# A state-space scan and its feed-forward on one core: the factors of the first pair, the scan and the decay matmuls put elsewhere

## The chip, the core and the metric

The kernel runs on one NeuronCore of a Trainium2 chip. A core has a matrix engine (TensorE, PE in the profile), a vector engine (VectorE, DVE), an activation engine (ScalarE, ACT), a general engine (GpSimd, POOL) and a queue engine (SyncE, SP). Each has its own instruction stream and they meet only at semaphores. Data lies in SBUF (128 partitions); matmul results go to PSUM, in eight banks. Loads and stores are DMAs that SP, ACT or POOL issue.

The metric is the device time of the whole kernel in microseconds (us): the median of eight runs.

## The reference

Two layers follow each other. The first is a chunked state-space recurrence over 4 batches of 8 heads, 768 steps, head size D = 32, state size N = 16. With `cum` the running sum of `log a` inside a chunk:

```python
L = np.exp(cum[:, :, :, None] - cum[:, :, None, :]) * causal
M = np.einsum('bhin,bhjn->bhij', Cc, Bc) * L
y = einsum('bhij,bhjd->bhid', M, xc) + einsum('bhin,bhnd->bhid', Cc, state) * np.exp(cum)[..., None]
state = decay_full * state + sum_j Bc[j] x[j] * decay_from_j[j]
```

Its output, 3072 tokens of 256 channels, goes through a gated feed-forward with 1536 hidden channels:

```python
gate = np.maximum(x @ w_gate, 0.0)
val = x @ w_val
return (gate * val) @ w_out
```

## The kernel before, in words

**Decays as factors.** The kernel does not form `L`. It takes running products of `a` (`cp0` for batch 0, `cp` for all batches), multiplies C by the product at its own step and B by its inverse, so that C times B carries the ratio. `factors()` (L213) turns `cp0`, one row per head and chunk of 128 steps, into a PSUM tile `fac` with steps on partitions, by matmuls against parts of the identity. L772 copies it to SBUF as `wfac[:, 1]` (the factors of C); reciprocals give `wfac[:, 0]` (the factors of B), pair 0 in L778, pairs 1 and 2 in L784. These serve batch 0.

For batches 1 to 3 `scan()` (L236) runs the products of all batches over half a sequence (384 steps) on VectorE. `middle()` (L242) takes the reciprocal of the product at half time, into `pick`. `decay()` (L249) turns it over: eight matmul records for the first pair of batch 1 (`dec3`, L257) and six for the rest (L262), in one PSUM bank; a float32 matmul is two records. `decay_factors()` (L269) copies the result to SBUF on ScalarE (`fac3`, `scaleBC`).

**Pairs and blocks.** Work on the recurrence goes by pairs of 128-step chunks, 256 tokens, three pairs to a batch, twelve in all. A pair's steps are: load B, C, x; scale B and C by the factors (`scale_wide`, L303; L322 is its product); transpose both on TensorE (`transp`); evacuate them as BT and CT (`tevac`, L369; CT is L385 on ScalarE or L388 on VectorE); multiply (`G_wide`, L411: 16 small matmuls into four PSUM banks); mask on VectorE (`gmask`, L433) with ScalarE copies (`gcopy`, L437); sum states (`adds`, `carry`, `pass_on`); multiply with state and x (`inter_wide` L498, `D_wide` L523); evacuate to `yT` (`yevac_wide`, L540). The feed-forward goes by blocks of 512 tokens, two pairs. `gvh` (L677) does one group of 128 hidden channels for half a block (four matmuls, L686; relu on ScalarE, L689; product on VectorE in `finish`, L692), `gv` (L663) one group for a whole block (L668, L671, L674, L675), `fout` (L699) the output matmuls (L713). `keep_warm` (L186) issues matmuls into a spare bank that nobody reads.

**PSUM banks.** The pool tag "shared" has five banks, used in turn. `gvh` takes one, `G_wide` four, `gv` two. A bank is free again when the last reader of its contents is done: for `gvh(..., True)` that is the `finish` that is called later in the program.

**Order.** The order of each engine is the order of the program: `in_order` (L15) ties every instruction to the one before it on its engine. The beginning of the program is therefore a hand-written order: pair 0 as fast as its inputs allow, pair 1 behind it, and from L838 on `gvh` groups of block 0 in between. The weights come through Pool's DMA queue in pieces of 128 hidden channels times two; their first issue waits for a one-element memset of `wg` on VectorE (L773). Between these issues Pool also scales pair 1 (L786, L787). Input loads are issued on SP and on ACT, in the order in which they are written (L132 to L144).

The stretch from L825 on, where the decay matmuls stand:

```python
f0 = gvh(0, 0, 0, True)
G_wide(1)
decay()
adds(1)
gcopy(1, 0)
gmask(1, 2, V, True)
f0()
```

Of the kernel before, what the change touches and what calls it, by code (L numbers as in the profile page):

```python
# [8 lines left out]
FP32 = mybir.dt.float32  # L9
# [20 lines left out]
def kernel(  # L30
# [13 lines left out]
    nc = tc.nc  # L44

    NB, NH, S, D = x.shape
# [15 lines left out]
    mm = ctx.enter_context(tc.tile_pool(name="mm", bufs=1, space=bass.MemoryType.PSUM))  # L62
# [14 lines left out]
    st = {}  # L77

    def load_bc(p, j, *qs):
        s = st.setdefault(p, {})  # L80
        if "bcr" not in s:
            s["bcr"] = raw.tile([128, NH, 2, 2, N], FP32, tag="bcr", name="bcr")
            if p == 2:
                nc.vector.memset(s["bcr"][0:1, 0, 1, 0, 0:1], 0.0)
        b, s0 = p // PPB, p % PPB * 256
        n = NH // len(qs)
        for i, q in enumerate(qs):
            hs = slice(i * n, (i + 1) * n)
            q.dma_start(
                out=s["bcr"][:, hs, j].rearrange("p h r n -> p h (r n)"),  # L90
                in_=(B, C)[j][b, hs, s0:s0 + 256, :].rearrange(
                    "h (p r) n -> p h (r n)", r=2))

    def load_x(p, *qs):
        xr = raw.tile([128, NH, 2, D], FP32, tag="xr", name="xr")
        if p == 2:
            nc.vector.memset(xr[0:1, 0, 0, 0:1], 0.0)
        b, s0 = p // PPB, p % PPB * 256
        n = NH // len(qs)
        for i, q in enumerate(qs):  # L100
            hs = slice(i * n, (i + 1) * n)
            q.dma_start(out=xr[:, hs].rearrange("p h r d -> p h (r d)"),
                        in_=x[b, hs, s0:s0 + 256, :].rearrange(
                            "h (p r) d -> p h (r d)", r=2))
        st.setdefault(p, {})["xr"] = xr
# [23 lines left out]
    H = S // 2  # L129
    HC = NC // 2  # L130
# [5 lines left out]
    nc.vector.memset(first, 0.0)  # L136
    load_bc(0, 1, nc.sync, nc.scalar)
    load_bc(0, 0, nc.sync, nc.scalar)
    a_sb = glob.tile([2 * BH, H], FP32)
    nc.sync.dma_start(out=a_sb, in_=a.rearrange("b h (w s) -> (b h w) s", w=2))  # L140
    load_x(0, nc.sync, nc.scalar)
    load_bc(1, 1, nc.sync)
    load_bc(1, 0, nc.scalar)
    load_x(1, nc.sync)  # L144
    nc.scalar.activation(first[:, 1:2], first[:, 0:1], AF.Relu)
# [9 lines left out]
    for rows, base in ((slice(0, 128), 128), (slice(0, 64), 0)):  # L155
        nc.gpsimd.affine_select(
            out=wmask[rows], in_=wmask[rows], pattern=[[-1, 2], [1, 128]],
# [28 lines left out]
    def keep_warm(n, rhs=warm):  # L186
        w = bank("w", (128, 128))
        for _ in range(n):
            nc.tensor.matmul(out=w, lhsT=warm, rhs=rhs, start=True, stop=True)  # L189
# [5 lines left out]
    def weights(f0, f1, which=(0, 1)):  # L195
        fs = slice(f0 * 128, f1 * 128)
        for j in which:
            w, src = ((wg, moe_w_gate), (wv, moe_w_val))[j]
            nc.gpsimd.dma_start(  # L199
                out=w[:, :, fs], in_=src[:, fs].rearrange("(k p) f -> p k f", k=2))  # L200
# [10 lines left out]
    dec = glob.tile([128, NC], FP32)  # L211

    def factors():  # L213
        d = bank("fac", (128, 2, NH, PPB))
        for r in range(2):
            for i in range(2):
                nc.tensor.matmul(
                    out=d[64 * i:64 * i + 64, r].rearrange("p h k -> p (h k)"),
                    lhsT=cp0[:, r:128:2], rhs=idr[:, i:R:2], start=(r == 0), stop=True,
                    tile_position=(0, 64 * i), skip_group_check=True)  # L220
        return d
# [3 lines left out]
    def decays(step):  # L225
        if step == 0:
            nc.vector.tensor_scalar_mul(ends, onew, cp0[:, 127:128])
            return
        d = bank("dec", (128, NC))
        nc.tensor.matmul(out=d, lhsT=heads.rearrange("p q t n -> p (q t n)"), rhs=ends,  # L230
                         start=True, stop=True)
        nc.scalar.copy(out=dec, in_=d)
# [3 lines left out]
    def scan(s0, s1):  # L236
        nc.vector.tensor_tensor_scan(
            out=cp[:, s0:s1], data0=a_sb[:, s0:s1],
            data1=zero1.to_broadcast([2 * BH, s1 - s0]),
            initial=cp[:, s0 - 1:s0] if s0 else 1.0, op0=ALU.mult, op1=ALU.add)  # L240

    def middle():  # L242
        nc.vector.reciprocal(rmid, cp[:, H - 1:H])
        nc.vector.tensor_scalar_mul(pick[:, 0], pairs[:, 0], rmid)

    fac3 = glob.tile([128, 2, 2, NH], FP32)
    scaleBC = glob.tile([128, NB, NC, 2, 8], FP32)

    def decay():  # L249

        bank_ = mm.tile([128, HC * 2 * NB * 8 + 16], FP32, tag="tp", name="dec")
        n = HC * 2 * NB * 8
        d = bank_[:, 0:n].rearrange("p (k w b h) -> p k w b h", k=HC, w=2, b=NB)
        st["dec3"] = d3 = bank_[:, n:n + 16].rearrange("p (r h) -> p r h", r=2)
        for r in range(2):
            for i in range(2):
                nc.tensor.matmul(  # L257
                    out=d3[64 * i:64 * i + 64, r], lhsT=cp[:, i * 128 + r:i * 128 + 128:2],
                    rhs=pick[:, 0, NH:2 * NH], start=(r == 0), stop=True,
                    tile_position=(0, 64 * i), skip_group_check=True)  # L260
        for k in range(HC):
            nc.tensor.matmul(  # L262
                out=d[:, k].rearrange("p w b h -> p (w b h)"),
                lhsT=cp[:, k * 128:(k + 1) * 128],
                rhs=pick.rearrange("p w h -> p (w h)"),
                start=False, stop=True, skip_group_check=True)
        st["dec"] = d

    def decay_factors():  # L269
        d = st["dec"]  # L270
        nc.scalar.copy(out=fac3[:, 1], in_=st["dec3"])
        for w in range(2):
            cs = slice(w * HC, (w + 1) * HC)
            nc.scalar.copy(
                out=scaleBC[:, :, cs, 1, :].rearrange("p b k h -> p k b h"), in_=d[:, :, w])

    def inverse(b0, b1):
        for b in range(b0, b1):
# [24 lines left out]
    def scale_wide(p, j, eng):  # L303
        s = st[p]
        if p >= FIRST:
            s["bs"] = bs = tok[p % NTOK]
            src = s["bcr"].rearrange("s (t q) j r n -> s j r t q n", t=2)[:, j]
            for t in range(2):
                k = 2 * j * (1 + t)
                eng.tensor_tensor(  # L310
                    out=bs[:, k:k + 2].rearrange("s k (q t n) -> s k t q n", q=4, t=2)[:, :, t],
                    in0=src[:, :, t],
                    in1=fac3[:, j, :, 4 * t:4 * t + 4].to_broadcast([128, 2, 4, N]),
                    op=ALU.mult)
            return
        if "bs" not in s:
            s["bs"] = bs = att.tile([128, 4, 128], BF16, tag="bs", name="bs")
            s["tin"] = [[bs[:, 2 * j + r] for r in range(2)] for j in range(2)]
        src = s["bcr"].rearrange("s (t q) j r n -> s j r t q n", t=2)[:, j]
        f = wfac[:, j, :, :, p]  # L320
        for t in range(2):
            eng.tensor_tensor(  # L322
                out=s["bs"][:, 2 * j:2 * j + 2].rearrange(
                    "s k (q t n) -> s k t q n", q=4, t=2)[:, :, t],
                in0=src[:, :, t],
                in1=f[:, :, 4 * t:4 * t + 4].to_broadcast([128, 2, 4, N]),
                op=ALU.mult)
# [101 lines left out]
    def gmask(p, q, eng, psum=False):  # L429
        s = st[p]  # L430
        d = s["gw"][:, q]
        m = (wmask if p < FIRST else wmask3).unsqueeze(2).to_broadcast([128, 2, 2, 128])
        eng.tensor_tensor(out=d, in0=s["gp"][q] if psum else d, in1=m, op=ALU.mult)  # L433
# [332 lines left out]
    V, A_, P_ = nc.vector, nc.scalar, nc.gpsimd  # L766

    keep_warm(22)
    d = factors()
    decays(0)  # L770
    keep_warm(8)
    nc.vector.tensor_copy(wfac[:, 1], d)  # L772
    nc.vector.memset(wg[0:1, 0, 0:1], 0.0)  # L773
    weights(0, 2)
    weights(2, 4)
    weights(4, 6, (0,))
    scale_wide(0, 1, V)
    nc.vector.reciprocal(wfac[:, 0, :, :, 0], wfac[:, 1, :, :, 0])  # L778
    scale_wide(0, 0, V)
    transp(0, 1, False)  # L780
    keep_warm(4)
    transp(0, 0, True)
    tevac(0, A_, V)
    nc.vector.reciprocal(wfac[:, 0, :, :, 1:3], wfac[:, 1, :, :, 1:3])  # L784
    scan(0, H)
    scale_wide(1, 1, P_)  # L786
    scale_wide(1, 0, P_)  # L787
    weights(4, 6, (1,))
# [12 lines left out]
    gmask(0, 1, V, True)  # L801
    pass_on(0, 0)
    carry(0, 0)
    middle()
    inter_wide(0)
    D_wide(0, (2, 3, 0))
    D_wide(0, (1,))
# [13 lines left out]
    def halves(b, u, *fs):  # L821
        for f in fs:
            gvh(b, f, u)

    f0 = gvh(0, 0, 0, True)  # L825
    G_wide(1)
    decay()
    adds(1)
    gcopy(1, 0)
    gmask(1, 2, V, True)  # L830
# [4 lines left out]
    pass_on(1, 0)  # L835
    gmask(1, 0, V)
    gmask(1, 1, V)
    late = [gvh(0, f, 0, True) for f in (1, 2, 3)]  # L838
    inter_wide(1)
    D_wide(1)  # L840
    late[0]()
    late[1]()
    yevac_wide(1, A_, V)
    late += [gvh(0, f, 0, True) for f in (4, 5)]
    for fin in late[2:]:
        fin()
    decay_factors()
    scale_wide(2, 1, P_)
    scale_wide(2, 0, P_)
    make_upper_triangular(nc, maskUT[:, 0], 1.0, diag=True)  # L850
# [6 lines left out]
    for t in tok:  # L857
# [1 line left out]
    wmask3 = const.tile([128, 2, 128], BF16)  # L859
    nc.gpsimd.tensor_copy(wmask3.rearrange("p k (r m) -> p k r m", r=2),  # L860
                          wmask.rearrange("p k (m r) -> p k r m", r=2))
    halves(0, 1, 0, 1, 2, 3, 4, 5)
    gv(0, 6)
    carry(1, 1)
    gv(0, 7)
# [164 lines left out]
```

## Time and profile before

| | us |
|---|---|
| median of 8 runs | 125.16 |
| lowest and highest run | 124.36 and 126.23 |
| profiled execution, its own time | 124.58 |
| its span in the trace | 122.9 |
| PE busy | 118.2 |
| DVE, ACT, POOL busy | 87.9, 76.2, 48.5 |

The granted TensorE clock was 1.00 throughout. A row of the timeline reads: start, time from the first start to the last end, engine, line, operation, output and input, count; in brackets how long the engine had been idle and what released it. A row of the chain reads: start, length, engine, output, line. A row of the DMA view gives its size and the time from issue to landing. In the rows an operation's length includes its start-up, and the next one on the same engine may begin a little before it ends.

### The profile page before, as it was taken

Reading aid. Unit: us, or ns where it says so; the run is one execution under the profiler, and the core shown is the slowest. Engines: PE = TensorE matmul, PEld = TensorE weight load, DVE = VectorE, ACT = ScalarE, POOL = GpSimd, SP = SyncE. Lnnn points to the kernel's source line nnn. Section 1 sums busy time; section 2 is a strip of 40 time slices with the busy share of each in tenths; the row PEclk is TensorE's granted clock in tenths of the full one; section 3 lists DMA queues with packets and bytes.
Section 4 is the critical chain, followed back from the end, with each engine's and each line's share of the span. In section 5 each row is a group of like instructions: output and inputs, shape, how many; then the busy total and the mean of one; then the engine's idle time right before and its main releaser. Section 6 shows DMA issues by size and latency. Waiting matters only on the chain.

```text
span 122.9 us, 3665 instructions
## 1 busy us (share of the span) xinstructions
PE 118.2 (96%) x1404; PEld 82.4 (67%) x1404; DVE 87.9 (72%) x200; ACT 76.2 (62%) x169; POOL 48.5 (39%) x108
## 2 busy tenths in 40 slices
PE   6989999999999999999999999999999999999990
PEld 6856785577775478874577864677854678844790
DVE  4798988872799864988763897855988656788410
ACT  0467688835887734786735886545877447876420
POOL 6499989572463327341181804233600033000000
DMA  3999999996979897999899998872580002200022
GB/s 63 208 214 138 171 185 196 189 163 96 117 92 151 111 137 192 109 109 213 110 138 137 161 159 135 100 106 40 189 51 0 0 0 91 85 0 0 5 85 85
DMA packets 77489, 13.93 MB, mean 113 GB/s; under 512 B 70064, under 2 KB 77472, under 8 KB 77472
## 3 DMA queue, kind: packets, MB, share of 16 engines
q1 hardware_dynamic: 70128, 10.61, 56.1%
q0 software_dynamic: 4288, 2.36, 14.2%
q10 hardware_dynamic: 3056, 0.72, 2.7%
q8 instruction: 11, 0.18, 0.6%
q14 instruction: 6, 0.05, 0.1%
HBM read 11.13 MB, written 3.15 MB: 116 GB/s over the span
## 4 chain that ended last, share of the span: by engine, by line
PE 92%; POOL 4%; DVE 1%; issue 1%; DVEq 0%
PE o L713 26%; PE gv L686 21%; PE val L671 15%; PE gate L668 15%; PE y L643 2%; PE g L548 2%; PE w L189 2%; POOL wg L199 2%; POOL bs L322 1%; PE y L632 1%; PE o L707 1%; PE A_ps L601 1%; PE g L418 1%; POOL wv L199 1%; PE y L523 1%; PE dec L262 1%
## 5 line engine op out<-in xcount | busy, mean ns | idle before, releaser
L675 DVE TENSOR_TENSOR h<-r,val 128x512 bf16<-128x512 bf16 x44 | 30.0, 684 | 7.4 <-ACT r L674 7.2
L713 PE MATMUL o<-wo,h 128*128 128x256 bf16 x276 | 33.1, 273 | 0.0
L674 ACT ACTIVATE r<-gate 128x512 bf16<-128x512 f32 x44 | 26.3, 597 | 9.7 <-PE gate L668 9.3
L713 PEld LDWEIGHTS <-h 128*128 128x128 bf16 x276 | 25.8, 98 | 5.3 <-issue 1.7
L668 PE MATMUL gate<-yT,wg 128*128 128x512 bf16 x88 | 26.2, 379 | 0.0
L671 PE MATMUL val<-yT,wv 128*128 128x512 bf16 x88 | 26.2, 379 | 0.0
L692 DVE TENSOR_TENSOR h<-r,gv 128x256 bf16<-128x256 bf16 x56 | 22.5, 419 | 2.6 <-ACT r L689 1.8
L689 ACT ACTIVATE r<-gv 128x256 bf16<-128x256 f32 x56 | 21.2, 385 | 2.3 <-PE gv L686 0.3
L686 PE MATMUL gv<-yT,wg 128*128 128x256 bf16 x112 | 21.6, 273 | 0.0
L686 PE MATMUL gv<-yT,wv 128*128 128x256 bf16 x112 | 21.4, 273 | 0.0
L556 POOL TENSOR_SCALAR_AFFINE_SELECT gs<-gs 128x512 bf16<-128x512 bf16 (+1 forms) x16 | 7.9, 521 | 28.8 <-ACT gs L567 28.8
L573 DVE TENSOR_TENSOR gs<-g,maskUT 128x512 bf16<-128x512 f32 x16 | 10.3, 686 | 11.4 <-issue 5.6
L338 POOL TENSOR_TENSOR tok<-bcr,scaleBC 128x128 bf16<-128x128 f32 x32 | 12.2, 407 | 15.2 <-DMA bcr<-in_B_dram 13.0
L671 PEld LDWEIGHTS <-wv 128*128 128x128 bf16 x88 | 8.6, 98 | 10.4
L668 PEld LDWEIGHTS <-wg 128*128 128x128 bf16 x88 | 8.6, 98 | 8.9
L686 PEld LDWEIGHTS <-wv 128*128 128x128 bf16 x112 | 11.0, 98 | 1.3
L686 PEld LDWEIGHTS <-wg 128*128 128x128 bf16 x112 | 10.2, 98 | 1.9 <-DVE yT L536 0.2
L567 ACT CAST gs<-g 128x512 bf16<-128x512 f32 x8 | 4.7, 589 | 6.7 <-PE g L548 6.7
L656 ACT CAST yT<-y 128x512 bf16<-128x512 f32 x8 | 4.7, 585 | 5.1 <-PE y L643 2.5
L433 DVE TENSOR_TENSOR gs<-g,wmask 128x512 bf16<-128x512 f32 x9 | 5.9, 681 | 2.7 <-PE g L418 2.7
L189 PE MATMUL w<-warm 128*128 128x128 bf16 x49 | 5.5, 282 | 1.1 <-DVE tmask L163 1.1
L189 PEld LDWEIGHTS <-warm 128*128 128x128 bf16 x58 | 5.0, 127 | 1.7 <-DVE tmask L163 1.1
(122 smaller groups left out, 116.3 us busy)
## 6 DMA issues: line engine op xcount, KB each, us to landing
xr<-in_x_dram SPq DMA_DIRECT2D x17, 128.0 KB, 3.3
out_dram<-ob SPq DMA_DIRECT2D x3, 512.0 KB, 3.4
bcr<-in_C_dram SPq DMA_DIRECT2D x17, 64.0 KB, 3.2
bcr<-in_B_dram SPq DMA_DIRECT2D x17, 64.0 KB, 3.1
out_dram<-ob SPq DMA_DIRECT2D x4, 256.0 KB, 2.8
xr<-in_x_dram SPq DMA_DIRECT2D x3, 256.0 KB, 3.9
wo<-in_moe_w_out_dram POOLq DMA_DIRECT2D x2, 384.0 KB, 9.1
wg<-in_moe_w_gate_dram POOLq DMA_DIRECT2D x4, 128.0 KB, 4.4
```

What stands on the lines that cost most here:

```text
L189: nc.tensor.matmul(out=w, lhsT=warm, rhs=rhs, start=True, stop=True)
L338: eng.tensor_tensor(out=dst[:, t, j * (1 + t)], in0=src[:, j, :, t], in1=f[:, j, :, 4 * t:4 * t + 4].to_broadcast([128, 2, 4, N]), op=ALU. ...
L556: nc.gpsimd.affine_select(out=dst, in_=dst, pattern=[[0, n], [1, 128]], compare_op=ALU.is_ge, fill=0.0, base=0, channel_multiplier=-1)
L573: nc.vector.tensor_tensor(out=d[:, q], in0=g[q], in1=m, op=ALU.mult)
L668: nc.tensor.matmul(out=g, lhsT=wg[:, k, fs], rhs=yT[:, k, tk], start=(k == 0), stop=(k == 1))
L671: nc.tensor.matmul(out=v, lhsT=wv[:, k, fs], rhs=yT[:, k, tk], start=(k == 0), stop=(k == 1))
L674: nc.scalar.activation(r, g, AF.Relu)
L675: nc.vector.tensor_tensor(out=fst[b][:, f], in0=r, in1=v, op=ALU.mult)
L686: nc.tensor.matmul(out=gv_[:, j], lhsT=w[:, k, fs], rhs=yT[:, k, tk], start=(k == 0), stop=(k == 1), skip_group_check=True)
L689: nc.scalar.activation(r, gv_[:, 0], AF.Relu)
L692: nc.vector.tensor_tensor(out=fst[b][:, f, u * 256:(u + 1) * 256], in0=r, in1=gv_[:, 1], op=ALU.mult)
L713: nc.tensor.matmul(out=o[:, ts % 2], lhsT=fst[b][:, f, ts * 128:(ts + 1) * 128], rhs=wo[:, f], start=(f == 0), stop=(f == NF - 1), skip_gr ...
```

## The change

Six things change place or form.

1. On SP, the load of `a` for all batches (`a_sb`) goes behind the loads of pair 0's x and pair 1's C.
2. Pair 0's C is scaled with the factors in PSUM (`fac`), and its B factors are the reciprocal of that; the copy of `fac` to SBUF goes to ScalarE, for pairs 1 and 2. Six `keep_warm` matmuls stand there instead of eight.
3. The memset that the first weights wait for comes directly behind `factors()`; `decays(0)`, one small product on VectorE, comes behind it.
4. The scan is cut in two halves of 192 steps: one behind `carry(0, 0)`, one behind pair 1's last mask. `middle()` follows the second, with its product on Pool. The finish of group 2 (`late[1]`) goes behind `yevac_wide(1)`.
5. `decay()` goes from the place behind `G_wide(1)` to behind three of pair 1's `gvh` groups, `decay_factors()` one group later.
6. The decay matmuls for batches 1 to 3 no longer cover batch 0: 48 columns instead of 64.

```diff
     load_bc(0, 0, nc.sync, nc.scalar)
+    load_x(0, nc.sync, nc.scalar)
+    load_bc(1, 1, nc.sync)
     a_sb = glob.tile([2 * BH, H], FP32)
     nc.sync.dma_start(out=a_sb, in_=a.rearrange("b h (w s) -> (b h w) s", w=2))
-    load_x(0, nc.sync, nc.scalar)
-    load_bc(1, 1, nc.sync)
     load_bc(1, 0, nc.scalar)
...
         nc.vector.reciprocal(rmid, cp[:, H - 1:H])
-        nc.vector.tensor_scalar_mul(pick[:, 0], pairs[:, 0], rmid)
+        nc.gpsimd.tensor_scalar_mul(pick[:, 0], pairs[:, 0], rmid)
...
-        bank_ = mm.tile([128, HC * 2 * NB * 8 + 16], FP32, tag="tp", name="dec")
-        n = HC * 2 * NB * 8
-        d = bank_[:, 0:n].rearrange("p (k w b h) -> p k w b h", k=HC, w=2, b=NB)
-        st["dec3"] = d3 = bank_[:, n:n + 16].rearrange("p (r h) -> p r h", r=2)
+        n = HC * 2 * (NB - 1) * NH
+        bank_ = mm.tile([128, n + 2 * NH], FP32, tag="tp", name="dec")
+        d = bank_[:, 0:n].rearrange("p (k w b h) -> p k w b h", k=HC, w=2, b=NB - 1)
+        st["dec3"] = d3 = bank_[:, n:].rearrange("p (r h) -> p r h", r=2)
...
-                out=d[:, k].rearrange("p w b h -> p (w b h)"),
-                lhsT=cp[:, k * 128:(k + 1) * 128],
-                rhs=pick.rearrange("p w h -> p (w h)"),
+                out=d[:, k].rearrange("p w b h -> p w (b h)"),
+                lhsT=cp[:, k * 128:(k + 1) * 128], rhs=pick[:, :, NH:],
                 start=False, stop=True, skip_group_check=True)
...
-                out=scaleBC[:, :, cs, 1, :].rearrange("p b k h -> p k b h"), in_=d[:, :, w])
+                out=scaleBC[:, 1:, cs, 1, :].rearrange("p b k h -> p k b h"), in_=d[:, :, w])
...
-        f = wfac[:, j, :, :, p]
+        f = fac[:, :, :, 0] if p == 0 and j else wfac[:, j, :, :, p]
...
     keep_warm(22)
-    d = factors()
-    decays(0)
-    keep_warm(8)
-    nc.vector.tensor_copy(wfac[:, 1], d)
+    fac = factors()
     nc.vector.memset(wg[0:1, 0, 0:1], 0.0)
     weights(0, 2)
     weights(2, 4)
     weights(4, 6, (0,))
+    decays(0)
+    keep_warm(6)
     scale_wide(0, 1, V)
-    nc.vector.reciprocal(wfac[:, 0, :, :, 0], wfac[:, 1, :, :, 0])
+    nc.vector.reciprocal(wfac[:, 0, :, :, 0], fac[:, :, :, 0])
+    nc.scalar.copy(out=wfac[:, 1], in_=fac)
     scale_wide(0, 0, V)
...
-    scan(0, H)
     scale_wide(1, 1, P_)
...
     carry(0, 0)
-    middle()
+    scan(0, H // 2)
     inter_wide(0)
...
     G_wide(1)
-    decay()
     adds(1)
...
     gmask(1, 1, V)
+    scan(H // 2, H)
+    middle()
     late = [gvh(0, f, 0, True) for f in (1, 2, 3)]
     inter_wide(1)
     D_wide(1)
     late[0]()
-    late[1]()
     yevac_wide(1, A_, V)
     late += [gvh(0, f, 0, True) for f in (4, 5)]
-    for fin in late[2:]:
+    for fin in late[1:]:
         fin()
-    decay_factors()
     scale_wide(2, 1, P_)
...
-    halves(0, 1, 0, 1, 2, 3, 4, 5)
+    halves(0, 1, 0, 1, 2)
+    decay()
+    halves(0, 1, 3)
+    decay_factors()
+    halves(0, 1, 4, 5)
```

## The prediction

> **What bounds the kernel now.** I read the chain that ended last first, then its front end in order of time, then VectorE's and ScalarE's rows for the first 15 us. Shares of the chain, by engine:
>
> ```profile
> PE 92%; POOL 4%; DVE 1%; issue 1%; DVEq 0%
> ```
>
> TensorE sets the end. The same chain in order of time (start, length, work) shows from where on:
>
> ```profile
> 8.54 1.73 POOL bs L322 x4
> ...
> 11.16 0.39 PE g L418 x16
> 11.55 0.34 PE dec L257 x8
> 11.89 0.81 PE dec L262 x6
> ...
> 12.88 1.42 PE gv L686 x12
> ...
> 14.97 3.60 PE gv L686 x32
> ```
>
> From 12.88 us on, TensorE hardly stops: 32 matmuls in 3.60 us are 0.1125 us each, as fast as these come anywhere, and so it stays to 119.9 us. Two rules follow. A start that is t earlier ends the kernel t earlier. TensorE work put behind 15 us costs its whole length; before that it may stand in a wait. VectorE's rows tell which waits there are:
>
> ```profile
> 4.19 0.21 DVE L772 COPY wfac<-fac 128x48 f32<-128x48 f32 x1 [0.71 <-PE fac L217]
> 4.34 0.06 DVE L773 MEMSET wg<- 1x1 bf16 x1
> 4.43 0.49 DVE L322 TENSOR_TENSOR bs<-bcr,wfac 128x128 bf16<-128x128 f32 x2
> 4.85 0.25 DVE L778 RECIPROCAL wfac<-wfac 128x16 f32<-128x16 f32 x1
> 5.13 0.49 DVE L322 TENSOR_TENSOR bs<-bcr,wfac 128x128 bf16<-128x128 f32 x2
> ...
> 6.40 0.89 DVE L237 TENSOR_TENSOR_SCAN cp<-a_sb,zero 64x384 f32<-64x384 f32 x1
> 7.21 1.26 DVE L433 TENSOR_TENSOR gs<-g,wmask 128x512 bf16<-128x512 f32 x2
> ...
> 11.66 0.69 DVE L433 TENSOR_TENSOR gs<-g,wmask 128x512 bf16<-128x512 f32 x1 [0.39 <-PE g L418]
> 12.27 0.41 DVE L692 TENSOR_TENSOR h<-r,gv 128x256 bf16<-128x256 bf16 x1
> ```
>
> The last two rows matter most. G_wide(1) on TensorE takes four of the five shared banks and gvh(0,0) the fifth. The next user, gvh(0,1), gets gvh(0,0)'s bank back when f0 (L692) ends at 12.27 + 0.41 = 12.68 us; it starts at 12.81. Between G_wide(1) and that moment TensorE has only decay() (11.48 to 12.62) and adds(1). The decay matmuls stand in a wait that exists without them.
>
> **The change, part by part.**
>
> *Pair 0's factors from PSUM.* The copy L772 and the memset leave the path of the first scaling: 4.43 to 4.19, 0.24 us. The trace has no product or reciprocal with factors in PSUM, so it has to be bounded. [...] I take the rows: the first reciprocal could end at 4.61 + 0.25 = 4.86. But the B of pair 0, which the next scaling (L322 at 5.13) needs, lands late: the SP queue's half was issued at 1.74 and took 3.3 us:
>
> ```profile
> bcr<-in_B_dram SPq DMA_DIRECT2D x1, 64.0 KB, 3.3
> ```
>
> That is 5.04 (1.74 + 3.3). So scaling B starts near 5.07 by either count, and 0.06 is left for it, CT, BT and G_wide(0) (6.42 to 6.36). ScalarE's new copy of wfac stands ahead of its BT copy (6.00); it needs some 0.2 us (L772's row) in an idle stretch from 4.46, even if it waits for the DVE reads until 4.9. The reciprocal for pairs 1 and 2 needs it at 6.08. Nothing.
>
> *Scan out of the first masks.* gmask(0,2) waits for the scan: 7.21. G_wide(1)'s own mask came 0.54 after its first matmul (11.12 to 11.66), so without the scan gmask(0,2) can start at 6.36 + 0.54 = 6.90: 0.31 earlier, and the last mask's end goes from 9.49 to 9.18. What then is late? D_wide(0) also waits for inter_wide(0), behind ScalarE's cast of x and Sw (8.60 + 0.31), a chain which hangs on G_wide(0) and gains 0.06: D_wide's first 24 matmuls start 9.13 instead of 9.19, and its last 8, which waited for the last mask until 9.54, follow at once at 9.38. D_wide(0) is 0.16 earlier. The half scan now ahead of DVE's yevac_wide(0): 128 columns took 0.60, 384 took 0.89, so 192 take 0.67; from 9.10 to 9.77, and yevac is due at 9.84. Hidden by 0.07.
>
> *Weights at once.* The memset that Pool's first weights wait for moves from 4.34 to about 3.30, behind L183. Pool starts at 3.62 instead of 4.73, its five issues (0.93, then four of 0.72) end at 7.42, and pair 1 is scaled by 9.15 instead of 10.27. The chain walks through Pool here, but what G_wide(1) waits for last is CT on ScalarE:
>
> ```profile
> 10.23 0.84 ACT L385 ACTIVATE CT<-tp,tmask 128x256 bf16<-128x256 bf16 x2
> ```
>
> It ends at 11.07 and the matmuls start at 11.12. It hangs on yevac_wide(0) and on the first transposes behind D_wide(0), not on Pool. So G_wide(1) gains D_wide's 0.16 and no more; what Pool wins is slack.
>
> *Loads.* On SP the a_sb issue (0.57 us) goes behind x0 and C of pair 1, both 0.57 earlier. a_sb is issued near 3.4; with the longest time of its neighbours (x of pair 1, 4.4) it lands by 7.8, wanted at 9.10. Weights' packets began near 7.2 for an issue at 4.73, so now near 6.1, beside x of pair 1, which has until 10.7. Nothing.
>
> *Decay out of its wait.* In front, gvh(0,1) comes at f0's end. f0 moves 0.16 with G_wide(1), to 12.52; with the 0.05 that TensorE's matmuls took after a mask (9.49 to 9.54) it starts 12.57 instead of 12.81: gain 0.24 in all, no more of the 1.15 us. TensorE then idles about 1 us there. Behind, decay() stands after three halves of pair 1 at near 17 us, in the dense stretch. Its eight d3 records cost 0.34 as before. The six others go from 64 to 48 columns: 8 columns took 201 ns and 64 took 272, 1.27 ns a column, so 16 fewer save 0.02 each, 0.12 of 0.81. With a switch at the ends, 0.34 + 0.69 + 0.02 = 1.05 us (0.9 if the column share is larger, 1.15 if loading weights sets the pace). That is added whole.
>
> *Scan's second half and middle().* On VectorE, after gmask(1,1) (end 13.97 by now): 0.6 for the scan, 0.2 for the reciprocal, 0.36 for late[0]; yevac_wide(1) starts at 15.12 where D_wide(1) would allow 14.88. Its yT is ready at 15.54; the first half of pair 1 would go at 15.53 and goes at 15.60: 0.07 lost (0 to 0.25). Banks for the halves follow: late[1] ends 15.86, wanted at 16.03; tight, but free. The pick product on Pool (SBUF products of 128 columns took 0.40 there, so 0.1 to 0.6, I take 0.3) stands behind the weights (through by 14.4) and ahead of scale_wide(2); it is done near 15.2, decay wants it at 16.9. The three ScalarE copies of decay_factors (0.57) go one half later; ScalarE has just gained 1 us on TensorE there.
>
> **Sum.** −0.24 + 0.07 + 1.05 = +0.88 us. The profiled execution took 124.58 (span 122.9 and 1.7 around it), so it would take 125.46. The median of the eight runs stands 0.58 above it; what that holds is left alone, so the median goes from 125.16 to **126.04**.
>
> **Rivals.**
> *A, decay covered.* If the halves of pair 1 wait for banks or for yT anyway, decay costs nothing. For it: VectorE is one product later there, at 0.39 us a product against 0.43 of TensorE. Against it: six products in 2.34 us outrun TensorE, and each bank was free 0.15 us ahead by my count. It decides if the halves are over 0.4 us late; wholly covered, 125.16 − 0.17 = 124.99. Not slower.
> *B, Pool was the gate.* The chain passes through it. If CT could follow Pool, G_wide(1) would come 1.11 earlier: −1.11 − 0.08 + 1.12 = −0.07, 125.1. Against it: the transposes of pair 1 stand behind D_wide(0) on TensorE.
> *C, both A and B*, or loads that hold back the median run and no longer do: −1.11 − 0.08 + 0.07 gives 124.04.
> *D, a_sb late.* VectorE stands on the half scan with yevac_wide(0) behind it. It decides once a_sb lands after 9.2, 1.4 later than computed, then one for one: 1 us more gives 127.0.
>
> **How the numbers follow.** The forecast 0.64, A 0.10, B 0.08, C 0.12, D 0.06. The forecast's own range is from −0.5 + 0.9 = +0.4 (B of pair 0 in time, so that the 0.24 and the masks' 0.31 pass on) to −0.1 + 1.15 + 0.25 = +1.3: 125.56 to 126.46. 0.5% is 0.63 us, about what a measurement of this kernel can tell from no change. Some 0.09 of the forecast's 0.64 lies under +0.63: same 0.09 + 0.10 + 0.08 = 0.27, faster 0.12, slower 0.61. The range reaches down to A and B and up to D's beginning: 124.9 to 126.8, with C's 0.12 and half of D outside.
>
> **What would show it.** First scaling at 4.19, second still near 5.07; gmask(0,2) near 6.9; G_wide(1) near 10.96; TensorE empty from about 11.5 to 12.57; dec rows near 17 us in the chain with 1.05 us; the matmuls of block 1 about 0.9 later. Wrong would be: G_wide(1) before 10.5, no hole ahead of gvh(0,1), or a wait in the halves that the dec rows fill.

## The result and the profile after

| | before | after |
|---|---|---|
| median, us | 124.86 (54 runs, with those shown first) | 126.36 (19 runs) |
| lowest run, us | 124.35 | 125.16 |
| profiled execution, us | 124.58 | 125.33 |
| its span, us | 122.9 | 123.5 |

The ratio of the two is 1.0081, with a 95% interval of 1.0053 to 1.0109: on 124.86 us, 1.0 us slower (0.7 to 1.4). The forecast was +0.88 us. 8 of the 19 runs of after, and 3 of the 54 of before, lie more than 1.5% above the fastest of their kernel; the ratio leaves them out, and no run tests whether the change makes them more frequent. The two profiled executions differ by 0.75 us in time and 0.6 us in span, and these are what the rows below are summed against; the remaining quarter of a microsecond shows in no row.

The chain of the changed kernel by engine, from its page: TensorE's share has gone up, and Pool is no longer in it.

```profile
PE 95%; ACT 2%; DVE 1%; issue 0%; DVEq 0%; ACTq 0%
```

The same chain in order of time (start, length, work), the stretch that answers to the one shown of before. Lines of the changed kernel are one lower in number from `scale_wide` on.

```profile
10.89 0.44 PE g L417 x16
11.32 0.58 ACT gs L436
11.91 0.04 issue
11.95 1.47 PE gv L685 x12
13.42 0.22 PE y L497 x8
13.64 0.27 PE Aps L497 x8
...
14.33 2.44 PE gv L685 x20
16.77 0.34 PE dec L257 x8
17.11 0.80 PE dec L262 x6
17.90 1.42 PE gv L685 x12
19.32 0.43 PE gate L667 x2
```

Two things are to be seen. (Group 6, `gate` in the rows, is the first `gv` group and comes behind all groups of `gvh`.) Behind the matmuls of G_wide(1) (g L417) the chain leaves TensorE for 0.62 us: it goes through ScalarE's copy of the first bank (L436), then into gvh(0,1). And the decay matmuls stand in the chain between two groups of gvh, with nothing beside them. `gate L667` starts at 19.32; before it started at 18.57.

VectorE's rows, which answer to those shown of before:

```profile
4.19 0.48 DVE L321 TENSOR_TENSOR bs<-bcr,fac 128x128 bf16<-128x128 f32 x2 [0.69 <-PE fac L217]
4.59 0.25 DVE L776 RECIPROCAL wfac<-fac 128x16 f32<-128x16 f32 x1
4.88 0.49 DVE L321 TENSOR_TENSOR bs<-bcr,wfac 128x128 bf16<-128x128 f32 x2
...
6.88 1.29 DVE L432 TENSOR_TENSOR gs<-g,wmask 128x512 bf16<-128x512 f32 x2 [0.64 <-PE g L417]
...
9.14 0.54 DVE L237 TENSOR_TENSOR_SCAN cp<-a_sb,zero 64x192 f32<-64x192 f32 x1
9.72 0.42 DVE L539 CAST yT<-Aps 128x256 bf16<-128x256 f32 x1
...
11.99 0.41 DVE L691 TENSOR_TENSOR h<-r,gv 128x256 bf16<-128x256 bf16 x1
...
13.78 0.60 DVE L237 TENSOR_TENSOR_SCAN cp<-a_sb,cp,zero 64x192 f32<-64x192 f32 x1
```

The front is what the change says: the factors are read from PSUM at 4.19, the first mask starts at 6.88 without a scan ahead of it, and both half scans sit between other work. One row contradicts the forecast: f0 (L691) ends at 11.99 + 0.41 = 12.40, yet gvh(0,1) ran from 11.95, and the row of TensorE names what it waited for:

```profile
11.95 0.38 PE L685 MATMUL gv<-yT,wg 128*128 128x256 bf16 x2 [0.50 <-ACT gs L436]
```

### The profile page after: what moved, and what is told of

Read it like the earlier page. It is cut to its first block, busy times and chain, and to the rows that moved or that the text cites. A ratio compares the mean times of both kernels' runs of the same rounds, so it can differ in the third digit from the quotient of the medians.

```text
span 123.5 us, 3662 instructions
## 1 busy us (share of the span) xinstructions
PE 118.3 (96%) x1402; PEld 82.3 (67%) x1402; DVE 87.2 (71%) x199; ACT 76.4 (62%) x170; POOL 49.0 (40%) x109
## 4 chain that ended last, share of the span: by engine, by line
PE 95%; ACT 2%; DVE 1%; issue 0%; DVEq 0%; ACTq 0%
PE o L712 25%; PE gv L685 21%; PE val L670 15%; PE gate L667 15%; PE w L189 3%; PE y L642 2%; PE g L547 2%; PE g L417 1%; PE y L631 1%; PE y L522 1%; PE o L706 1%; PE A_ps L600 1%; ACT gs L436 1%; PE dec L262 1%; PE Aps L497 1%; PE fac L217 0%
## 5 line engine op out<-in xcount | busy, mean ns | idle before, releaser
L667 PE MATMUL gate<-yT,wg 128*128 128x512 bf16 x88 | 26.2, 379 | 0.0
L691 DVE TENSOR_TENSOR h<-r,gv 128x256 bf16<-128x256 bf16 x56 | 22.2, 417 | 3.6 <-ACT r L688 3.0
L667 PEld LDWEIGHTS <-wg 128*128 128x128 bf16 x88 | 8.6, 98 | 8.9
```

The costliest lines, as they stand in the source:

```text
L667: nc.tensor.matmul(out=g, lhsT=wg[:, k, fs], rhs=yT[:, k, tk], start=(k == 0), stop=(k == 1))
L691: nc.vector.tensor_tensor(out=fst[b][:, f, u * 256:(u + 1) * 256], in0=r, in1=gv_[:, 1], op=ALU.mult)
```

## Where the time went

Where TensorE's rows start at five places, in us of the two profiled executions:

| start of | before | after | gained so far |
|---|---|---|---|
| G_wide(1) | 11.12 | 10.85 | 0.27 |
| gvh(0,1) | 12.81 | 11.95 | 0.86 |
| gvh(0,4), behind D_wide(1) | 14.91 | 14.26 | 0.65 |
| first half of pair 1 | 15.79 | 15.28 | 0.51 |
| gate of group 6 (in the chain) | 18.57 | 19.32 | −0.75 |

So 0.27 us was won at the front and another 0.59 from the matmuls that left the place behind G_wide(1). Of this 0.86, 0.21 went ahead of D_wide(1) and 0.14 ahead of pair 1's first half. The decay matmuls, with the change from one kind of matmul to another on either side, then cost 0.51 + 0.75 = 1.26 us.

## The experiments

### Only the decay matmuls moved

```diff
     G_wide(1)
-    decay()
     adds(1)
...
-    decay_factors()
     scale_wide(2, 1, P_)
...
-    halves(0, 1, 0, 1, 2, 3, 4, 5)
+    halves(0, 1, 0, 1, 2)
+    decay()
+    halves(0, 1, 3)
+    decay_factors()
+    halves(0, 1, 4, 5)
```

with the 48 columns of after, everything else as before.

> Before, with only the decay matmuls (48 columns) and the copies of their result moved behind three groups of pair 1. Theory 1 (the place behind G_wide(1) covers half of them, the new place nothing): gvh(0,1) near 12.2 instead of 12.81, since its bank comes free with the first ScalarE copy of G_wide(1), some 0.2 us of that lost again ahead of D_wide(1), then 1.2 us added: +0.7 to +0.9 us over before. Theory 2 (as predicted: gvh(0,1) waits for f0): gvh(0,1) near 12.75, +1.0 to +1.2 us. Rival A (halves wait anyway): -0.4 to -0.6 us.

Measured: ratio to before 1.0070 (1.0042 to 1.0098), 0.87 us. TensorE's rows of its timeline:

```profile
11.39 0.21 PE L457 MATMUL y<-xb,bs 64*32 64x64 bf16 x4
...
12.14 0.38 PE L685 MATMUL gv<-yT,wg 128*128 128x256 bf16 x2 [0.50 <-ACT gs L436]
```

The hole behind adds(1) is 0.50 us and ends with ScalarE's copy, at 11.51 + 0.58 in this run's chain, not with f0. So the bank that gvh(0,1) takes is the first of G_wide(1)'s four, which gcopy(1, 0) sets free, and gvh(0,1) came 0.67 us earlier than in before (0.08 of it because G_wide(1) was earlier). The decay matmuls had been half covered in their old place: they took 1.14 us and held TensorE up by 0.6. In the chain of the same run the groups and the decay behind them:

```profile
14.52 2.29 PE gv L685 x20
16.80 0.34 PE dec L257 x8
17.15 0.80 PE dec L262 x6
```

This one move gives nearly the whole of the result (1.0070 against 1.0081; the intervals overlap almost fully). It also shows where after's front gain went: gvh(0,1) is 0.19 us later here than in after, but the decay matmuls start at 16.80 against 16.77. The twenty matmuls ahead of them take 2.29 us here and 2.44 in after, where the second half scan makes yT late.

### The decay matmuls twice

```diff
     halves(0, 1, 0, 1, 2)
     decay()
+    decay()
```

> After, with the decay matmuls issued twice at their new place; the second time writes the same values. Theory 1 (that place covers nothing): the second fourteen records cost their whole length, +1.1 to +1.2 us over after, so about +1.8 to +2.1 over before. Rival A (the groups there wait for banks or yT): under 0.4 us over after.

Measured: 1.0184 (1.0130 to 1.0239) of before, so 1.03% or 1.3 us over after. Its chain:

```profile
16.84 0.34 PE dec L257 x8
17.18 0.81 PE dec L262 x6
17.99 0.04 issue
18.03 0.41 PE dec L257 x8
18.44 0.80 PE dec L262 x6
19.23 1.42 PE gv L685 x12
```

The second set goes from 18.03 to 19.23, 1.20 us, with no wait taken away elsewhere. The new place covers nothing; rival A falls.

### Only the front

```diff
...
-        f = wfac[:, j, :, :, p]
+        f = fac[:, :, :, 0] if p == 0 and j else wfac[:, j, :, :, p]
...
-    d = factors()
-    decays(0)
-    keep_warm(8)
-    nc.vector.tensor_copy(wfac[:, 1], d)
+    fac = factors()
     nc.vector.memset(wg[0:1, 0, 0:1], 0.0)
...
+    decays(0)
+    keep_warm(6)
     scale_wide(0, 1, V)
-    nc.vector.reciprocal(wfac[:, 0, :, :, 0], wfac[:, 1, :, :, 0])
+    nc.vector.reciprocal(wfac[:, 0, :, :, 0], fac[:, :, :, 0])
+    nc.scalar.copy(out=wfac[:, 1], in_=fac)
```

> Before, with only the front of the change: pair 0 scaled from PSUM, six warm matmuls, weights at once. Loads, scan, middle and decay stay where they were. Theory 1 (the front gains 0.1 to 0.3 us, since masks and ScalarE's chain both hang on the first scalings): the first scaling at 4.19, the first mask near 6.95 behind the scan, G_wide(1) 0.15 to 0.27 us earlier than 11.12, time 0.15 to 0.3 us under before. Rival (Pool is the gate of pair 1): G_wide(1) about 1 us earlier, time 0.9 to 1.1 us under before.

Measured: 0.9981 (0.9952 to 1.0010), that is 0.24 us under before in the middle and not told from nothing. In its profiled execution G_wide(1) starts at 11.16, no earlier than before, so the rows do not bear out the expected gain. Two things hold it, and they end within 0.1 us of each other, so the rows cannot say which alone would. The first: with before's order of loads and the weights at once, pair 1's C was late (5.0 us to landing, 3.9 in before). The second: G_wide(0) is slow in this execution (0.65 us from 6.47, 0.42 from 6.42 in before), and the first mask waits for it.

```profile
8.70 1.58 POOL L322 TENSOR_TENSOR bs<-bcr,wfac 128x128 bf16<-128x128 f32 x4 [1.23 <-DMA bcr<-in_C_dram]
...
7.28 1.29 DVE L433 TENSOR_TENSOR gs<-g,wmask 128x512 bf16<-128x512 f32 x2 [0.17 <-PE g L418]
```

Pool is free at 7.47, a microsecond earlier than in before, and then stands 1.23 us for that load, so it has pair 1 scaled at 10.28, as in before (10.26). The masks start at 7.28 (7.21 in before), and pair 0's yT is ready on VectorE at 10.45 (10.42). This run therefore says nothing on rival B, since Pool was no earlier. After does: there Pool had pair 1 scaled at 9.24, a microsecond earlier, and G_wide(1) gained 0.27 us, where the rival asked for 0.9 to 1.1. Moving C ahead of a_sb, the first part of the change, is what lets Pool start at 7.47 in after: C was issued at 3.05 there and landed 4.0 us later.

### The weights' release back

```diff
-    nc.vector.memset(wg[0:1, 0, 0:1], 0.0)
-    weights(0, 2)
-    weights(2, 4)
-    weights(4, 6, (0,))
     decays(0)
     keep_warm(6)
     scale_wide(0, 1, V)
+    nc.vector.memset(wg[0:1, 0, 0:1], 0.0)
+    weights(0, 2)
+    weights(2, 4)
+    weights(4, 6, (0,))
```

in after, the rest unchanged.

> After, with only the weights' release moved back behind the scaling of pair 0's C. Theory (Pool has 0.4 us of slack in after, not 1.1): Pool starts near 4.95, has pair 1 scaled near 10.5, G_wide(1) near 11.2 instead of 10.85, time 0.2 to 0.4 us over after. Rival (Pool hides): time as after.

Measured: 1.0125 (1.0085 to 1.0164) of before, 0.44% or 0.5 us over after, but the intervals overlap. Its profiled execution took 127.45 us against a median of 126.2, and its rows cannot be set beside after's: TensorE kept half its pace until past 12.8 us (the hardware section has the numbers), and G_wide(1) came at 12.76. That early weights are worth some tenths in after is likely and not shown.

### The decay matmuls in two waits of TensorE

```diff
     nc.vector.reciprocal(wfac[:, 0, :, :, 1:3], wfac[:, 1, :, :, 1:3])
+    scan(0, H // 2)
...
     carry(0, 0)
-    scan(0, H // 2)
+    scan(H // 2, H)
...
     carry(0, 1)
+    middle()
...
     adds(1)
+    decay(0, 1)
...
-    scan(H // 2, H)
-    middle()
     late = [gvh(0, f, 0, True) for f in (1, 2, 3)]
+    decay(1, HC)
...
-    halves(0, 1, 0, 1, 2)
-    decay()
-    halves(0, 1, 3)
+    halves(0, 1, 0)
     decay_factors()
-    halves(0, 1, 4, 5)
+    halves(0, 1, 1, 2, 3, 4, 5)
```

where `decay(k0, k1)` issues the d3 records only with k0 = 0 and the others for the given range, and a_sb is loaded ahead of pair 0's x again.

> After, with the scan's first half ahead of the first masks (where VectorE sat idle 0.64 us; a_sb loaded early again), its second half behind carry(0,0), middle() behind carry(0,1), and the decay matmuls divided between two waits of TensorE: eight plus two records behind adds(1), four ahead of inter_wide(1). Theory 1 (both places are waits in after): the records behind adds(1) cost about 0.1 us, the four others 0.1 to 0.3 us, and the 1.23 us of the late place are gone, as is the 0.15 us wait for yT: 1.0 to 1.3 us under after, 0.2 to 0.6 us under before. Rival (the sum of TensorE's work decides, wherever it stands): within 0.3 us of after.

Measured: 1.0053 (1.0020 to 1.0087), 0.35 us under after, with intervals that overlap: a third of what I expected. Its front did what it was to do. TensorE's rows:

```profile
11.43 0.41 PE L259 MATMUL dec<-pick,cp 64*64 64x8 f32 x8
11.77 0.42 PE L264 MATMUL dec<-pick,cp 64*128 64x48 f32 x2
12.12 0.39 PE L687 MATMUL gv<-yT,wg 128*128 128x256 bf16 x2
...
13.54 0.64 PE L264 MATMUL dec<-pick,cp 64*128 64x48 f32 x4
...
31.33 0.42 PE L419 MATMUL g<-turned 32*64 32x256 bf16 x16 [0.66 <-DMA turned<-tok]
```

The ten records behind adds(1) hold gvh(0,1) up by 0.17 us against after, the chain reaches group 6 at 18.46 (19.32 in after), and the 0.86 us are there. Then TensorE stands 0.66 us ahead of G_wide(3), whose transposed data come from a DMA that the loads of pair 3 start. In the kernel before, the weight load of G_wide(3) already waited 0.32 us for them, covered by the matmuls ahead of it: that kernel is just at this second gate, and a front that is earlier gains nothing there so long as pair 3 is not earlier too. But the gate itself has also moved. The transposing DMA was issued at the same time in both kernels, 27.72 and 27.69, and took longer to land; in before and here:

```profile
turned<-tok SPq DMA_TRANSPOSE x1, 3.1
...
turned<-tok SPq DMA_TRANSPOSE x1, 3.6
```

G_wide(3) starts at 30.84 in before and at 31.33 here, which is the whole 0.5 us between the two spans (122.9 and 123.4). Why the DMA takes longer is open.

### Earlier loads for the second gate

Pair 3's loads one group of block 0 earlier, on the kernel just shown:

```diff
     gv(0, 6)
+    load_x(2, nc.sync)
+    load(3)
     carry(1, 1)
     gv(0, 7)
-    load_x(2, nc.sync)
-    load(3)
```

> As in_waits, with the loads of pair 3 (and pair 2's x) written one group of block 0 earlier. In in_waits TensorE stood 0.66 us ahead of G_wide(3) for pair 3's transposed data, which hang on these loads; up to there it was 0.1 us ahead of before. Theory 3 (that chain of loads is a second gate and swallows what the front wins): the 0.66 us wait goes, G_wide(3) near 30.7, time 0.5 to 0.7 us under in_waits, 0 to 0.2 us under before. Rival (the transfer itself is late, from traffic): the wait stays, time as in_waits.

Measured: 1.0091 (1.0059 to 1.0123): not faster than the kernel that it starts from, and if anything slower. SP's queue shows that the order was not the limit:

```profile
21.96 2.81 SPq L89 DMA_DIRECT2D bcr<-in_B_dram  x1
24.82 0.81 SPq L102 DMA_DIRECT2D xr<-in_x_dram  x1
```

SP stands 2.81 us on the issue of B, where it stood 1.92 in the kernel before, and x follows at 24.82 instead of 24.27. In after, where the same loads are issued 0.75 us later than in before, the issue of B stands 0.93 us and ends at 23.98 (24.23 in before). The DMA share in this stretch, from 20 to 25 us, is above 1 (1.16 in before, 1.33 in the kernel just shown, 1.34 here), and the earlier request stood longer.

The rise over the kernel just shown is not put down to the loads of pair 3, though. This execution had lost 0.64 us before they were issued: G_wide(0) took 0.61 us instead of 0.42, pair 1's C took 5.3 us to land instead of 4.4, and G_wide(1) came at 11.53 instead of 10.89.

The same with pair 1's C moved up on SP and a_sb on ScalarE's queue:

```diff
-    a_sb = glob.tile([2 * BH, H], FP32)
-    nc.sync.dma_start(out=a_sb, in_=a.rearrange("b h (w s) -> (b h w) s", w=2))
     load_x(0, nc.sync, nc.scalar)
+    a_sb = glob.tile([2 * BH, H], FP32)
+    nc.scalar.dma_start(out=a_sb, in_=a.rearrange("b h (w s) -> (b h w) s", w=2))
     load_bc(1, 1, nc.sync)
```

> As waits_loads, with a_sb loaded through ScalarE's queue, so that pair 1's C is issued directly behind pair 0's x on SP. In in_waits Pool stood 0.62 us for pair 1's C (landed 8.09), and pair 1's B was scaled at 10.1. Theory 4 (weights at once delay pair 1's C unless its load is moved up, and then Pool is the gate): Pool scales pair 1 from 7.5 us on, G_wide(1) comes 0.2 to 0.3 us earlier than in in_waits (10.89), time 0.2 to 0.3 us under waits_loads, 0.3 to 0.5 us under before. Rival: G_wide(1) unchanged, time as waits_loads.

Measured: 1.0039 (1.0016 to 1.0061). Pool did start at 7.46, as theory 4 said, and the time is 0.6 us under the last one's. But G_wide(1) came at 11.21, later than in the kernel with the old loads (10.89). The first half scan waited for a_sb until 6.67, so that the first mask started at 7.21. G_wide(0), slow again (0.65 us from 6.39), would have held it about as long: in the run before, with a_sb in time, the mask started at 7.18. The expectation of a time under before was wrong.

The same loads with the front alone, scan and decay as before:

> As front_only (scan and decay as in before), with pair 1's C issued directly behind pair 0's x, a_sb through ScalarE's queue and pair 3's loads one group earlier. Theories 3 and 4: both gates gone, G_wide(1) near 10.9 to 11.0 instead of 11.2, decay behind it, time 0.2 to 0.3 us under front_only. Rival: time as front_only.

Measured: 1.0086 (1.0047 to 1.0125), where front_only had 0.9981. Its runs spread from 124.97 to 127.49. What costs it this is open: the same two changes of the loads took the kernel with the decay in two waits from 1.0053 to 1.0039, so neither is a likely culprit by itself.

### The transposing DMA ahead of pair 4's loads

```diff
-    load(4, ((0, "BC"),))
     turn_dma(3)
+    load(4, ((0, "BC"),))
```

on the kernel with the decay in two waits.

> As in_waits, with one line moved: the loads of pair 4's B and C go behind pair 3's transposing DMA on SP instead of ahead of it. Moving pair 3's loads earlier did not help (waits_loads): SP stood longer on the issue of B, 2.8 us instead of 1.9, so it is traffic and not the order to load that sets their end. Theory 5 (the transpose, issued at 27.7 and landed 3.6 us later, queues behind pair 4's loads that land at 29.3 to 29.7): it lands in 2 to 2.6 us, TensorE's 0.66 us wait ahead of G_wide(3) is gone or under 0.2 us, time 0.4 to 0.6 us under in_waits. Rival (the transpose takes that long by itself): no change.

Measured: 0.9993 (0.9958 to 1.0028), 0.6% under the kernel that it starts from (the intervals just overlap), as the theory asked. The mechanism did not show, though. Its profiled execution took 126.75 us, far from its median, so the rows are taken from the next kernel, which has the line moved too:

```profile
27.49 1.31 SPq L300 DMA_TRANSPOSE turned<-tok  x1
28.86 0.57 SPq L124 DMA_DIRECT2D bcr<-in_B_dram  x1
...
31.17 0.42 PE L419 MATMUL g<-turned 32*64 32x256 bf16 x16 [0.34 <-DMA turned<-tok]
```

With pair 4's loads behind it the transpose still took 3.6 us to land (27.49 to 31.13 in the chain), and TensorE still waited 0.34 us. So the theory that it queues behind those loads falls; why the time went down is open.

### Pair 1's C on ScalarE's queue

```diff
-    load_bc(1, 1, nc.sync)
+    load_bc(1, 1, nc.scalar)
...
-    load_bc(1, 0, nc.scalar)
+    load_bc(1, 0, nc.sync)
```

on the last kernel, and on the front alone with the transposing DMA moved.

> As turn_first, with the queues of pair 1's loads exchanged: C on ScalarE's queue, B on SP's. Theory 4 (weights at once make pair 1's C late on SP, so that Pool starts at 8.1 instead of 7.5): Pool scales pair 1 from 7.5 us on, G_wide(1) 0.2 us earlier than in turn_first, time 0.1 to 0.3 us under it and 0.2 to 0.5 us under before. Rival: B is then as late as C was, Pool ends at the same time, no change.

Measured: 0.9985 (0.9959 to 1.0012), 124.89 us in the median, its runs between 124.59 and 125.28. Pool scaled C at 7.47 but then stood 0.66 us for B: the rival was right that B becomes as late as C was. G_wide(1) at 10.81.

> As front_only (scan, middle and decay as in before), with the same exchange of queues and the transposing DMA of pair 3 ahead of pair 4's loads. Both theories: G_wide(1) near 10.9 to 11.0, decay behind it hides all but 0.6 us of itself as in before, no wait ahead of G_wide(3): 0.2 to 0.4 us under before, equal to or up to 0.2 us above waits_best. Rival: as front_only, 0.2 us under before.

Measured: 0.9975 (0.9933 to 1.0017), with runs from 124.13 to 130.0; its profiled execution is far from the median and is not read.

Both are level with before as far as this can be told, and both are about 1% faster than after. None of the eleven kernels is clear of before on the fast side.

## Why the prediction was right, step by step

**The bound.** TensorE, dense from 12.88 us to the end, a start earlier by t worth t. Right up to one point: ahead of G_wide(3) the kernel was already waiting for pair 3's data. The forecast did not look for such a place behind 15 us. It did not matter for after, which arrives there 0.75 us late and waits for nothing; 0.11 us of what comes back by the end of its span comes back there, where before stood waiting.

**Factors from PSUM.** First scaling 4.19 as computed. The reads from PSUM cost nothing that the rows show: the first pair of products took 0.48 us with the factors in PSUM and 0.49 with them in SBUF, the reciprocal 0.25 in both. That the reciprocal could end as early as 4.86 was the author's estimate, since no row of before has a product or reciprocal that reads factors from PSUM; it ended at 4.59 + 0.25 = 4.84. The second scaling came at 4.88, not 5.07: the forecast had it wait for the SP half of B until 5.04, whatever the reads from PSUM would cost, and in this execution that half landed at 1.75 + 2.9 = 4.65, so the whole 0.25 us passed on. Yet G_wide(0) moved only from 6.42 to 6.29; the hardware section says why.

**Scan out of the masks.** First mask 6.88 (computed 6.90), D_wide(0) 9.06 (9.13). The half scan took 0.54 us instead of 0.67. G_wide(1) 10.85 instead of 10.96, a gain of 0.27 where 0.16 was forecast.

**Weights and loads.** Pool started at 3.66 (3.62), had pair 1 scaled at 9.24 (9.15), a_sb landed at 7.4 (7.8 at the latest). "Nothing" was right for the loads as they stand in after. Without C's move it would have been wrong for Pool: front_only shows 1.23 us of waiting there.

**Decay out of its wait: the step that failed.** The forecast had gvh(0,1) held by f0, because five banks used in turn would give it gvh(0,0)'s. The rows show it held by gcopy(1, 0): with five banks used in turn it could not have started before f0 ended at 12.40, and it started at 11.95. So "used in turn", in the description of the kernel, does not hold; the bank came from the first release that the program has behind G_wide(1). What misled the forecast was before itself, where gvh(0,1) starts 0.13 us after f0's end. TensorE's rows there have no wait at all at this point; gvh(0,1) simply follows decay() and adds(1):

```profile
11.82 0.88 PE L262 MATMUL dec<-pick,cp 64*128 64x64 f32 x6
...
12.68 0.20 PE L458 MATMUL Aps<-xb,bs 64*32 64x64 bf16 x4
12.81 0.39 PE L686 MATMUL gv<-yT,wg 128*128 128x256 bf16 x2
```

So TensorE's wait without decay() was 0.5 us and not 1, the old place had covered only half of the decay matmuls, and gvh(0,1) came at 11.95 instead of 12.57. A gain of 0.86 us stood where the sum had 0.24.

**The price behind.** 1.05 forecast, 1.26 between the places in the table, 1.20 for the second set in the run with two. The mis-sized term is the columns, in the rows of the tile dec in after (number, then least, median and greatest length in ns, and when they start):

```profile
L262 PEld LDWEIGHTS dec<-pick,cp x6: 183/188/188, 17.0 to 17.6; 64*128 64x128 f32 x6
L262 PE MATMUL dec<-pick,cp x6: 272/272/307, 17.0 to 17.6; 64*128 64x48 f32 x6
```

Before, the same six with 64 columns had medians of 188 and 272 ns too, and held the chain 0.81 us against 0.80 now. What sets their pace is not the columns; the weight loads, unchanged at 188 ns, are the candidate that the forecast named for its upper bound, and no run tests them. The 1.27 ns a column came from comparing two forms that differ in their weights too: 64 columns of weights in the d3 records, 128 in the others. This makes 0.11 us of the 0.21. Most of the rest stands at the ends: the first record starts at 16.69, 0.31 us behind the start of the last two gvh matmuls, where the next two would follow at 0.22, and the forecast had 0.02 for both ends.

**Second half scan.** The wait for yT was 0.14 us where 0.07 was computed. What the sum had nothing for is the 0.21 us ahead of D_wide(1): with gvh(0,1) so early, inter_wide(1) is at TensorE before ScalarE has its state ready (13.22 + 0.35 = 13.57, and L497's second group starts at 13.62).

**The sum.** Forecast −0.24 + 0.07 + 1.05 = +0.88. In the rows −0.86 + 0.21 + 0.14 + 1.26 = +0.75 at group 6, of which 0.15 comes back by the end of the span. Two errors of opposite sign, 0.62 us at the bank and 0.49 behind it (0.21 at D_wide(1), 0.07 at yT, 0.21 in the price), nearly cancel. That the sum came so close is luck. The direction rested on the one step that held: matmuls in the dense stretch cost their whole length, which two runs confirm (1.14 us for the fourteen records in the chain of decay_late, 1.20 for the second set in that of decay_twice).

**Rivals.** A (decay covered) falls with decay_twice. B (Pool the gate) falls in the size it was given: in after Pool was a microsecond earlier and G_wide(1) 0.27 us. D did not occur, a_sb was 1.7 us early. C falls with A and B, and nothing else got faster.

## What to carry to other kernels

Before moving filler work out of a wait, find out what ends that wait, and by which release: here the bank pool gave the next user a bank that was released earlier than the one expected, so half of the supposed hole was not there. In before the start of gvh(0,1) lay next to two ends, f0's and decay()'s, and only removing one told which counted. Work that left a half-covered place for a dense one paid in full here (1.26 us), and what it freed was not all kept: 0.35 of 0.59 us was lost again at the next two things that had been hidden. And look for the next gate down the line before counting a front gain: a load chain that was just in time can swallow it.

## What the runs showed of the hardware

**In these profiled executions TensorE started at half its later pace, the step to full pace came at a different moment from one to the next, and the granted clock of 1.00 does not show it.** In before the 22 `keep_warm` matmuls from 1.07 us on take 2.52 us, 0.115 each, and two of the same form at 10.60 take 0.11, 0.055 each. Two kernels of the experiments, the one with the decay in two waits and the one with pair 3's loads earlier, are the same program up to about 18 us. Their G_wide(0) and first mask:

```profile
6.18 0.42 PE L419 MATMUL g<-CT,BT 32*64 32x256 bf16 x16
6.76 1.29 DVE L434 TENSOR_TENSOR gs<-g,wmask 128x512 bf16<-128x512 f32 x2
...
6.40 0.61 PE L419 MATMUL g<-CT,BT 32*64 32x256 bf16 x16
7.18 1.29 DVE L434 TENSOR_TENSOR gs<-g,wmask 128x512 bf16<-128x512 f32 x2 [0.54 <-PE g L419]
```

The scalings of pair 0 start at the same times in both, 4.19 and 4.88; the masks are 0.42 us apart, which is the size of the effects that these experiments look for. In after the transposes of pair 0's B were still slow (0.40 us from 5.43, where before has 0.28 from 5.67), which is why the 0.25 us of the scalings became 0.13 at G_wide(0). In the execution of 127.45 us (the weights' release back) the half pace lasted past 12.8 us: the four matmuls of gvh(0,0) and the step to G_wide(1) took 0.94 us, from 11.82 to 12.76, where after took 0.56. The granted clock reads 1.00 in all of these. What sets the moment of the step no run tests. A single profile can therefore be 0.4 us off at the front, as with the two masks, and more where the half pace lasts, as in the execution of 127.45 us.

**With the weights released earlier on Pool's queue, an older load on SP's queue took longer to land.** In the profiled execution of front_only, with the weights 1.1 us earlier and no other load moved, pair 1's C, issued from SP at 3.51 as in before, took 5.0 us to land instead of 3.9. In two further kernels with early weights and this order of loads it took 4.4 and 5.3.
